# Attention before two MoE layers: one pool of four PSUM banks, an order written out step by step, and a joint tile for the last queries of two heads

## The chip, the cores and the metric

The kernel runs on one core of a Trainium2 chip, in one launch. The metric is the device time of that launch in microseconds. Three runs of the kernel before took 1164.0 us in the median (1159.83 to 1167.98).

## The reference

The inputs are `q`, `k` and `v` of shape (2, 8, 576, 64), and the weights of two mixture-of-experts layers. Only the attention is touched by the change:

```
q_rot, k_rot = (rotate(q), rotate(k))          # rotary embedding, halves of 32
scores = scale * q_rot @ k_rot^T               # scale = 1/8
scores = scores - max(scores)
attn = exp(scores)
attn = attn / (sum(attn) + 1e-09)
out = attn @ v                                 # 2 batches x 8 heads x 576 x 64
```

The output is laid out as 1152 tokens x 512 and goes through the first MoE layer (8 experts, 512 to 1024 to 512, weights from a Sinkhorn iteration) and the second (144 tokens per expert).

## The kernel before, in words

Everything is in fp32 or fp32r. The attention takes the first 180 us or so of the span, and the first MoE layer, the second and the output follow. The 16 (batch, head) pairs are worked on as 8 pairs `P` of two heads `h`; a group `g` = 2P + h is one head. The 576 queries of a head are five tiles, four of 128 queries and one of 64. All 576 keys of a head are scored at once.

For one head the steps are these.

- **Rotation** (`rot`, L1230 to 1254). Four tensor_tensor instructions turn the raw q or k of a pair; they run on GpSimd (`POOL` in the profile), and on VectorE (`DVE`) for the first pair and for the q of the second. q is written twice side by side: the second copy is a DMA on SyncE's queue, or a ScalarE (`ACT`) copy for pair 0.
- **Transposes of q and k** (`tq`, L1267). 15 TensorE (`PE`) transposes fill two PSUM banks called `T`; ACT copies one (L1277) and DVE the other (L1278) to the tile `qk`.
- **Scores of a tile** (`score`, L1282). Two matmuls of 64 rows each write a tile `S` of two banks; an fp32 matmul is two instructions in the trace. DVE takes the negated maximum (L1290), ACT the exponential with its row sum (L1293). There are two `S` tiles, so that the scores of tile n+2 wait for the exponential of tile n.
- **Transposes of the exponentials** (`te`, L1301). Ten transposes of 64 rows fill two `T` banks (five and one bank for the tile of 64 queries); ACT copies the first bank to `pt` (L1311) and DVE the second (L1317).
- **Output** (`pv`, L1319). For a pair, two halves `c` of 288 queries, each five steps over the keys by two heads, into the one bank `PV`; the steps are split three and two. `norm` (L1349) multiplies by the spread reciprocals `rs` on DVE.
- **Reciprocals** (`rcp` L1327, `rbc` L1338). DVE inverts the sums, GpSimd spreads them (for the last pair ACT), nine transposes put them into two `T` banks, and ACT and DVE copy them out. `xsplit` (L1355) splits the result into high and low parts.

Eight PSUM banks are in use: four for the two `S` tiles, three `T` banks that are given out in turn, one `PV`. The order of issue comes from a list of times: within a group each step has a number (`SC` L1463, the tile's index plus 0.1 for `te` and so on), and the steps are issued sorted by it (L1459). `WARM` (L1464) puts filler matmuls of 128x128 by 512 in bf16 into the first steps. Each engine runs its own list in that order.

```
def bank():
    return ps.tile([128, 512], F32, name="T", bufs=3)
...
SC = dict(tq=1.5, rk=0.6, rq=2.6, rcp=4.4, rbc=0.5, pva=2.5, pvb=4.5, n=0.25, xs=0.35)
WARM = (6, 2, 2)
```

The first MoE layer's weights are loaded and converted beside the last pair (`open1`, `wconv`, `WC`), and its first steps (`m1.step`, matmuls of L682 and L701, gate matmuls of L615) stand among the last pieces of the attention.

Of the kernel before, what the change touches and what calls it, by code (L numbers as in the profile page):

```python
# [1134 lines left out]
WC = (0.6, 1.6, 3.6)  # L1135


def attention(tc, nc, ps, pss, lp, q, k, v, rope, ident, xH, xL, m1):
    with ExitStack() as st:
# [56 lines left out]
        tcs = pone.tile([128, 11, 64], F32, name="tcs")  # L1196
        load_k(nc.sync, 0, (0,), False)
# [3 lines left out]
        G.memset(raw["k"][:, :, 4:6, :], 0.0)  # L1201
        G.memset(raw["q"][64:128, :, 4, :], 0.0)
        for t in vs:
            G.memset(t[64:128, 4], 0.0)
        load_k(nc.sync, 0, ())
        load_q(A, 0, ())
        load_k(nc.sync, 0, (1,), False)
        load_q(nc.sync, 0, (1,), False)
        load_v(0)
        load_v(1)  # L1210
        sums = [one.tile([128, 2, 5], F32, name=f"sum{i}") for i in range(2)]
        for t in sums:
            V.memset(t, 1.0)
        wb = one.tile([128, 512], BF, name="wb")
# [8 lines left out]
        def warm(n):  # L1223
            p = ps.tile([128, 512], F32, name="PV", bufs=1)
            for _ in range(n):
                T.matmul(p, wb[:, 0:128], wb, start=True, stop=True)

        T1 = {}

        def rot(P, n, hs=(0, 1), e=G, dup=None):  # L1230
            x, tb = raw[n], tab[n]
            J = SL[n]
            U = 2 if n == "q" else 1
            if hs[0] == 0:
                T1[n, P] = ptwo.tile([128, 2, J, U, HD], F32, name="t1" + n)
                T1[n] = pone.tile([128, 2, J, HD], F32, name="t2" + n)
            t2 = T1[n]
            o = slice(hs[0], hs[-1] + 1)
            t1 = T1[n, P][:, o, :, 0]
# [4 lines left out]
            e.tensor_tensor(t2[:, o, :, 0:32], x[:, o, :, 32:64], table(64, 96), op=OP.mult)  # L1244
# [279 lines left out]
```

## Time and profile before

| | us |
|---|---|
| median of three runs | 1164.0 |
| the profiled execution | 1162.72 |
| its span | 1160.8 |
| PE busy | 1117.1 (96%) |
| DVE busy | 776.6 (67%) |
| ACT busy | 373.0 (32%) |
| POOL busy | 443.1 (38%) |
| first score matmul of pair 0 | at 13.37 |
| first matmul of the first MoE layer | at 178.26 |

How to read it: PE is TensorE's matmuls, PEld its weight loads, which run ahead of the matmuls and so show where TensorE's list stands still. A row of the timeline gives start and duration, engine, source line, what is written from what, the count of merged instructions, and in brackets the idle time before with what ended it. The ends of matmuls are modelled, so that PE shows as busy also while it drains.

### The profile page before, as it was taken

The numbers are of one execution on the slowest core, as the hardware profiler recorded it, in microseconds if no ns is written. First come the engines' busy times: TensorE is split into PE (matmuls) and PEld (weight loads), VectorE is DVE, ScalarE is ACT, GpSimd is POOL, SyncE is SP. The second block draws the span as 40 slices with busy tenths as digits, with TensorE's granted clock in tenths as the row PEclk, the third lists the DMA queues.
The fourth block names the chain that finished last, engine by engine and source line by source line (L and its number), as shares of the span: only waits on it lengthen the run. The fifth ranks groups of instructions, "written<-read, shape, count | busy, mean of one in ns | idle before, by whom it ended". The sixth has DMA issues, their size and how long they took to land. (4 is left out here: it accounts for less than half of the span.)

```text
span 1160.8 us, 20699 instructions
## 1 busy us (share of the span) xinstructions
PE 1117.1 (96%) x8133; PEld 969.4 (84%) x8133; DVE 776.6 (67%) x1732; ACT 373.0 (32%) x853; POOL 443.1 (38%) x429
## 2 busy tenths in 40 slices
PE   5889899999999999999999999999999999999997
PEld 3655557899898888888888898889889887999997
DVE  6677772365667777777777777666678888888200
ACT  4566663223422322223232333223331110222222
POOL 3767515215543443434444354434310000464111
PEclk9799999999999999999999999999999999999999
DMA  3322222200323242232423223111130003978830
GB/s 90 81 54 55 53 85 82 70 1 2 100 64 92 73 123 96 82 91 73 135 83 91 82 93 99 37 37 44 66 134 19 21 1 132 319 256 298 261 98 21
DMA packets 105297, 107.21 MB, mean 92 GB/s; under 512 B 35440, under 2 KB 68592, under 8 KB 105072
## 3 DMA queue, kind: packets, MB, share of 16 engines
q1 hardware_dynamic: 102448, 100.64, 28.0%
q0 software_dynamic: 2048, 4.72, 1.3%
q8 instruction: 64, 1.05, 0.4%
q10 hardware_dynamic: 704, 0.52, 0.2%
q14 instruction: 33, 0.27, 0.1%
HBM read 98.85 MB, written 4.72 MB: 89 GB/s over the span
## 5 line engine op out<-in xcount | busy, mean ns | idle before, releaser
L929 DVE SCALAR_TENSOR_TENSOR acc<-Y,pw,acc 128x512 f32<-128x512 f32 x216 | 158.2, 742 | 1.5 <-PE Y L927 0.4
L865 PE MATMUL T<-xH,wa 128*128 128x256 f32 (+1 forms) x576 | 137.6, 294 | 0.8 <-ACT v L885 0.8
L865 PEld LDWEIGHTS T<-big,wb 128*128 128x128 f32 x864 | 125.8, 188 | 10.7 <-DVE v L878 1.7
L878 DVE TENSOR_TENSOR v<-T,v 128x256 f32<-128x256 f32 (+1 forms) x240 | 108.1, 450 | 38.2 <-PE T L865 35.3
L865 PE MATMUL T<-big,wb 128*128 128x256 f32 (+1 forms) x864 | 133.1, 296 | 0.0
L865 PEld LDWEIGHTS T<-xH,wa 128*128 128x128 f32 x576 | 100.0, 188 | 8.7 <-ACT v L885 3.0
L682 PE MATMUL T<-xH,wa 128*128 128x384 f32 x336 | 93.0, 338 | 0.0
L774 POOL TENSOR_TENSOR wa<-wraw,wa 128x512 fp32r<-128x512 f32 (+1 forms) x48 | 48.8, 1019 | 105.0 <-ACT wa L773 105.0
L865 PE MATMUL T<-xL,wa 128*128 128x256 f32 (+1 forms) x288 | 84.5, 293 | 0.0
L1290 DVE TENSOR_REDUCE negmax<-S 128x1 f32<-128x576 f32 (+1 forms) x80 | 60.2, 752 | 36.2 <-PE S L1288 33.9
L872 DVE SCALAR_TENSOR_TENSOR hlB<-v,hhB 128x320 fp32r<-128x320 f32 x72 | 57.0, 792 | 38.7 <-ACT hhB L871 38.7
L871 ACT ACTIVATE hhB<-v 128x320 fp32r<-128x320 f32 x72 | 34.0, 472 | 136.4 <-DVE v L878 136.4
L871 ACT ACTIVATE hhA<-v 128x256 fp32r<-128x256 f32 x72 | 30.1, 418 | 148.4 <-DVE v L878 148.4
L927 PE MATMUL Y<-wa,hhB 128*128 128x512 f32 x240 | 75.3, 395 | 0.0
L927 PE MATMUL Y<-wb,hhB 128*128 128x512 f32 x240 | 75.1, 394 | 0.0
L872 DVE SCALAR_TENSOR_TENSOR hlA<-v,hhA 128x256 fp32r<-128x256 f32 x72 | 50.6, 703 | 35.3 <-ACT hhA L871 35.3
L1000 DVE SCALAR_TENSOR_TENSOR fr<-fr,fc 128x512 f32<-128x512 f32 x64 | 52.5, 820 | 32.3 <-DMA fr<-in_moe_w 32.3
L793 POOL TENSOR_TENSOR wb<-wraw,wb 128x512 fp32r<-128x512 f32 x24 | 30.6, 1299 | 102.0 <-ACT wb L792 102.0
L701 PE MATMUL Y<-wb,hh 128*128 128x512 f32 x216 | 68.8, 400 | 0.0
L793 POOL TENSOR_TENSOR wa<-wraw,wa 128x512 fp32r<-128x512 f32 x24 | 30.6, 1300 | 99.4 <-ACT wa L792 99.4
L1288 PE MATMUL S<-qk 64*128 64x288 f32 x320 | 62.2, 469 | 4.7 <-ACT big L1293 4.7
L1293 ACT ACTIVATE big<-S,negmax 128x576 f32<-128x576 f32 (+1 forms) x80 | 59.1, 738 | 19.2 <-DVE negmax L1290 15.6
(293 smaller groups left out, 2653.5 us busy)
## 6 DMA issues: line engine op xcount, KB each, us to landing
wraw<-in_moe_w SPq DMA_DIRECT2D x52, 512.0 KB, 5.4
fr<-in_moe_w SPq DMA_DIRECT2D x64, 256.0 KB, 4.1
wraw<-in_moe_w SPq DMA_DIRECT2D x48, 256.0 KB, 3.3
big<-in_moe_w SPq DMA_DIRECT2D x20, 512.0 KB, 4.5
wa<-in_moe_w SPq DMA_DIRECT2D x18, 512.0 KB, 5.0
wb<-in_moe_w SPq DMA_DIRECT2D x14, 512.0 KB, 4.9
fc<-in_moe_w_gate SPq DMA_DIRECT2D x9, 256.0 KB
ysc<-acc SPq DMA_DIRECT2D x9, 256.0 KB, 2.1
```

Source lines behind the costliest of these rows:

```text
L682: nc.tensor.matmul(p[:, :CH], w[:, wi, kt, (fb % 2) * 128:(fb % 2) * 128 + 128], x[:, kt, o], start=(n == 0), stop=(n == 11))
L701: nc.tensor.matmul(self.Y[c][t], a[:, o], w[:, wi, fb % 2], start=(fb == 0 and n == 0), stop=(fb == FB - 1 and n == 2))
L793: G.tensor_tensor(d["W"][:, 1, h], r[:, 2 + h], d["W"][:, 0, h].bitcast(F32), op=OP.subtract)
L865: nc.tensor.matmul(bank[:, 0:n], d[t][:, ww, b, r * 128:(r + 1) * 128], x(xw, r), start=(first and i == 0), stop=(i == 5), skip_group_chec ...
L871: A.activation(HH[:, f, o], src, AF.Relu)
L872: V.scalar_tensor_tensor(HL[:, f, o], src, 0.0, HH[:, f, o].bitcast(F32), op0=OP.max, op1=OP.subtract)
L878: V.tensor_tensor(o, bank[:, 0:n], x, op=OP.add)
L927: nc.tensor.matmul(y, h[:, f, o], w[:, ww, f], start=(f == 0 and z == 0), stop=(f == 1 and z == 2))
L929: V.scalar_tensor_tensor(self.acc[:, t], y, self.pw[:, t, e:e + 1], self.acc[:, t], op0=OP.mult, op1=OP.add)
L1288: T.matmul(p[:, a, :288], QK[g][o, i * 128:(i + 1) * 128], QK[g][o, 640:928], start=True, stop=True)
L1290: V.tensor_reduce(m[0:n], p[0:n, :, :288], axis=AX.XY, op=OP.max, negate=True)
L1293: pexp.append(lambda: A.activation(e[0:n, :576].rearrange("p (a c) -> p a c", a=2), p[0:n, :, :288], AF.Exp, bias=m[0:n], scale=1.0, accum ...
```

## The change

- **One pool of four banks.** The three `T` banks and the `PV` bank are taken once and kept in a list `free`. Every user (`tq`, `te`, `rbc`, each half of the output) takes the bank that was freed first, and gives it back where its copy is issued. While the eighth pair is finished, bank 0 is kept out for the MoE layer.
- **Order written out.** A string `ORDER` names the steps of one turn, one turn per pair; `<` and `>` mean the pair before and the pair after. Maximum, exponential and the two copies are steps of their own. The three-and-two steps of an output half stand between transposes of different tiles. `AFTER` says behind which steps the MoE layer's conversions and its first step are issued.
- **Nine tiles per pair in place of ten.** Tiles 0 to 3 are head 0, tiles 4 to 7 head 1, tile 8 holds the last 64 queries of head 0 in partitions 0 to 63 and of head 1 in 64 to 127. Its scores are four matmuls of 64 rows by 64 columns (L1326). Its maximum, exponential and copies are as for any other tile. The spread of its reciprocals is two 64x64 matmuls in place of a transpose (L1384), and two small copies.
- **First rotations.** Head 0 of pair 0 is rotated on VectorE, then at once head 1's k there and its q on GpSimd; pair 1 is rotated on GpSimd before anything else there, where it was k on GpSimd and q on VectorE among the tiles. The raw q and k have two buffers each. Filler: 14 matmuls at the start in place of 6 and 2, memset on GpSimd, and 2 behind each tile of pair 0.

```diff
-        raw = {n: pone.tile([128, 2, SL[n], HD], F32, name="raw" + n) for n in "qk"}
+        raw = {(n, i): pone.tile([128, 2, SL[n], HD], F32, name=f"raw{n}{i}") for n in "qk" for i in range(2)}
...
-        def bank():
-            return ps.tile([128, 512], F32, name="T", bufs=3)
+        bank = [ps.tile([128, 512], F32, name="T", bufs=3) for _ in range(3)]
+        bank.append(ps.tile([128, 512], F32, name="PV", bufs=1))
+        free = [0, 1, 2, 3]
+        own = []
+        hold = {}
+
+        def take(key, n):
+            hold[key] = [free.pop(0) for _ in range(n)]
+            return [bank[i] for i in hold[key]]
+
+        def give(key, r):
+            if hold[key][r] not in own:
+                free.append(hold[key][r])
...
+        def sc(P, i):
+            p = SS[P, i] = pss.tile([128, 2, 512], F32, name="S")
+            for a in range(2):
+                o = slice(64 * a, 64 * a + 64)
+                if i < 8:
+                    x = QK[P, i // 4]
+                    T.matmul(p[:, a, :288], x[o, i % 4 * 128:i % 4 * 128 + 128], x[o, 640:928], start=True, stop=True)
+                else:
+                    for h in range(2):
+                        x = QK[P, h]
+                        T.matmul(p[64 * h:64 * h + 64, a, :288], x[o, 512:576], x[o, 640:928], start=True, stop=True)
...
+        def rbc(P):
+            p = take(("r", P), 2)
+            d = RD["x", P]
+            for j in range(4):
+                halves(p, j, lambda o: d[o, 2 * j:2 * j + 2].rearrange("p h d -> p (h d)"))
+            for r in range(2):
+                o = slice(64 * r, 64 * r + 64)
+                T.matmul(p[r][o, 256:320], d[o, 8], ident[o, o], start=True, stop=True)
...
-        rot(0, "k", (0,), V)
-        V.memset(wb, 0.0)
-        rot(0, "q", (0,), V, copy)
-        warm(WARM[0])
-        tq(0)
-        rot(0, "k", (1,), V)
-        rot(0, "q", (1,), G, copy)
...
+        rot(0, "k", (0,), V, 0)
+        rot(0, "q", (0,), V, 1)
+        twice(0, 0, True)
+        rot(0, "k", (1,), V, 0)
+        rot(0, "q", (1,), G, 0)
+        load_q(nc.sync, 2, (0, 1))
+        load_k(nc.sync, 2, (0, 1))
+        rq(1)
+        rk(1)
+        warm(WARM[0])
+        for p in range(-1, NP + 3):
+            if p == NP and m1:
+                own = [0]
+                free = [i for i in free if i]
+            for w in ORDER.split():
+                f = w.rstrip("<>")
+                P = p + w.count(">") - w.count("<")
...
+                if f == "tq1" and P == 0:
+                    twice(0, 1, True)
...
+                if x == "te" and P == 0:
+                    warm(WARM[1])
...
-SC = dict(tq=1.5, rk=0.6, rq=2.6, rcp=4.4, rbc=0.5, pva=2.5, pvb=4.5, n=0.25, xs=0.35)
-WARM = (6, 2, 2)
+WARM = (14, 2)
+NC, QB = 9, 3
+ORDER = """sc0 te7< mx0 sc1 pa7< pb7< te8< ex0 pv01<< mx1 pa8< pb8< ex1 tq1 nm0<< lv sc2 qb1 qa1 te0 mx2 sc3 pa0
...
```

The whole order of TensorE in one turn is: sc0 te7 sc1 te8 pv01 tq1 sc2 te0 sc3 te1 pv10 rbc sc4 te2 sc5 te3 pv11 sc6 te4 tq0 sc7 te5 sc8 te6 pv00 (`tq0` for the pair after; te7, te8, `pv` and `rbc` for pairs before). `pv10` is the first three key steps of half 1, `pv11` its last two. ACT's is pa7 ex0 pa8 ex1 qa1 pa0 ex2 pa1 ex3 ra pa2 ex4 pa3 ex5 pa4 ex6 qa0 pa5 ex7 pa6 ex8, and DVE's is mx0 pb7 mx1 pb8 nm0 qb1 mx2 pb0 den mx3 pb1 rb mx4 pb2 mx5 pb3 nm1 mx6 pb4 qb0 mx7 pb5 mx8 pb6 (`pa`, `pb`: the copies of the two banks of a `te`; `qa`, `qb`: those of a `tq`; `ra`, `rb`: those of the spread reciprocals; `mx`, `ex`: maximum, exponential; `nm`: the product with the reciprocals).

TensorE in the middle of a pair, before. `T<-ident,big` is a `te`, `T<-ident,t1q` and `t1k` a `tq`, `T<-ident,rcp` the `rbc`:

```order
L1288 MATMUL S<-qk 128x288 x2
L1265 MATMUL T<-ident,big_100 128x64 x10
L1265 MATMUL T<-ident,rcp 128x64 x9
L1288 MATMUL S<-qk 128x288 x2
L1265 MATMUL T<-ident,big_100 128x64 x10
L1265 MATMUL T<-ident,t1q 128x64 x10
L1265 MATMUL T<-ident,t1k 128x64 x5
L1288 MATMUL S<-qk 128x288 x2
L1265 MATMUL T<-ident,big_99 128x64 x10
```

TensorE after, before the `tq` of a pair's head 1 (here PV and T are two banks of the one pool):

```order
L1322 MATMUL S<-qk 128x288 x2
L1289 MATMUL T<-ident,big_102 128x64 x10
L1361 MATMUL T<-pt_531,big_104 64x288
L1361 MATMUL T<-pt_670,big_104 64x288
L1361 MATMUL T<-pt_531,big_104 64x288
L1361 MATMUL T<-pt_670,big_104 64x288
L1289 MATMUL PV<-ident,t1q 128x64
L1289 MATMUL T<-ident,t1q 128x64
```

Where a `te` was followed at once by `rbc` or `tq`, which take two more of three banks, output matmuls now stand between.

TensorE after, the joint tile of the last queries:

```order
L1322 MATMUL S<-qk 128x288 x2
L1289 MATMUL T<-ident,big_102 128x64 x10
L1326 MATMUL S<-qk 64x288 x4
L1289 MATMUL T<-ident,big_103 128x64
L1289 MATMUL PV<-ident,big_103 128x64
```

Two tiles of `S` with two matmuls each have become one with four of half the width.

VectorE in the first steps, before (the four rotations of head 0's q, the copy of the first `tq`, the rotations of head 1's k):

```order
L1244 TENSOR_TENSOR t2q<-rawq,tabq 128x5x32
L1245 TENSOR_TENSOR t2q<-rawq,tabq 128x5x32
L1246 TENSOR_TENSOR rawq<-rawq,tabq 128x320
L1247 TENSOR_TENSOR t1q<-rawq,t2q 128x5x64
L1278 COPY qk<-T 128x7x64
L1244 TENSOR_TENSOR t2k<-rawk,tabk 128x6x32
L1245 TENSOR_TENSOR t2k<-rawk,tabk 128x6x32
L1246 TENSOR_TENSOR rawk<-rawk,tabk 128x384
L1247 TENSOR_TENSOR t1k<-rawk,t2k 128x384
```

VectorE in the first steps, after:

```order
L1245 TENSOR_TENSOR t1q<-rawq,t_101 128x5x64
L1242 TENSOR_TENSOR t_101<-rawk_97,tabk 128x6x32
L1243 TENSOR_TENSOR t_101<-rawk_97,tabk 128x6x32
L1244 TENSOR_TENSOR rawk_97<-rawk_97,tabk 128x384
L1245 TENSOR_TENSOR t1k<-rawk_97,t_101 128x384
L1307 COPY qk<-T 128x7x64
```

The copy that the first scores need has moved behind the rotation of head 1's k.

## Rows read from the trace of the kernel before

**Rows 1.** The page: busy time, share of the span, instructions of each engine
```profile
PE 1117.1 (96%) x8133; PEld 969.4 (84%) x8133; DVE 776.6 (67%) x1732; ACT 373.0 (32%) x853; POOL 443.1 (38%) x429
```

**Rows 2.** Busy time by stretch (columns: PE, PEld, DVE, ACT, POOL, granted clock, DMA)
```profile
29.00:57.00 28.00, 23.93 (x246) 17.35 (x246) 18.38 (x33) 17.05 (x44) 20.58 (x17) 0.76 0.34 84
57.00:76.80 19.80, 17.81 (x213) 11.62 (x211) 14.04 (x27) 12.84 (x32) 13.05 (x11) 1.00 0.16 36
```

**Rows 3.** Timeline of PE: first scores of pairs 1, 2, 7; first MoE matmul; first gate
```profile
34.09 1.27 PE L1288 MATMUL S<-qk 64*128 64x288 f32 x4
56.96 0.76 PE L1288 MATMUL S<-qk 64*128 64x288 f32 x4
155.83 0.76 PE L1288 MATMUL S<-qk 64*128 64x288 f32 x4
178.26 0.45 PE L682 MATMUL T<-xH,wa 128*128 128x384 f32 x1
192.68 0.33 PE L615 MATMUL T<-xH,gg 128*16 128x384 f32 x1
```

**Rows 4.** Timeline of PE's weight loads over the first head of a pair
```profile
96.50 0.30 PEld L1288 LDWEIGHTS S<-qk 64*128 64x128 f32 x4 [0.44 <-issue]
97.34 0.31 PEld L1288 LDWEIGHTS S<-qk 64*128 64x128 f32 x4
98.33 0.68 PEld L1324 LDWEIGHTS PV<-pt,big 128*64 128x64 f32 x8
99.45 0.30 PEld L1288 LDWEIGHTS S<-qk 64*128 64x128 f32 x4 [0.44 <-ACT big L1293]
100.76 0.60 PEld L1265 LDWEIGHTS T<-ident,rcp 64*128 64x128 f32 x9 [0.38 <-POOL rcp L1334]
101.28 0.31 PEld L1288 LDWEIGHTS S<-qk 64*128 64x128 f32 x4
102.38 0.39 PEld L1265 LDWEIGHTS T<-ident,big 64*128 64x128 f32 x9 [0.60 <-ACT rs L1347]
103.38 0.33 PEld L1265 LDWEIGHTS T<-ident,t1q 64*128 64x128 f32 x8 [0.61 <-ACT pt L1311]
104.75 0.38 PEld L1265 LDWEIGHTS T<-ident,big 64*128 64x128 f32 x9 [0.44 <-ACT qk L1277]
105.20 1.17 PEld L1324 LDWEIGHTS PV<-pt,big 128*64 128x64 f32 x12
106.80 0.30 PEld L1288 LDWEIGHTS S<-qk 64*128 64x128 f32 x4 [0.44 <-issue]
```

**Rows 5.** Waits of PE's weight loads over five pairs (57 to 156): total, times, longest
```profile
PEld T L1265 <- ACT pt L1311: 7.5, 15, 0.7
PEld T L1265 <- ACT qk L1277: 5.5, 10, 0.7
```

**Rows 6.** Groups by line over the same five pairs: maximum, exponential, reading of its sum
```profile
L1290 DVE TENSOR_REDUCE negmax<-S 128x1 f32<-128x576 f32 (+1 forms) x50 | 37.6, 753 | 24.0 <-PE S L1288 21.7 <-PE T L1265 2.2
...
L1293 ACT ACTIVATE big<-S,negmax 128x576 f32<-128x576 f32 (+1 forms) x50 | 36.9, 738 | 6.6 <-DVE negmax L1290 4.1
...
L1293 ACT ACTIVATION_READ_ACCUMULATOR big<-S,negmax 128x1 f32 (+1 forms) x50 | 9.7, 194 | 0.0
```

**Rows 7.** Timeline of the first 18 us: rotations on DVE, first copy, scores 0 to 3
```profile
9.71 1.03 DVE L1247 TENSOR_TENSOR t1q<-rawq,t2q 128x320 f32<-128x320 f32 x1
...
12.44 0.62 DVE L1278 COPY qk<-T 128x448 f32<-128x448 f32 x1 [1.70 <-PE T L1265]
...
13.37 2.29 PE L1288 MATMUL S<-qk 64*128 64x288 f32 x8
13.63 0.56 DVE L1246 TENSOR_TENSOR rawk<-rawk,tabk 128x384 f32<-128x384 f32 x1
...
16.42 0.76 PE L1288 MATMUL S<-qk 64*128 64x288 f32 x4 [0.76 <-ACT big L1293]
...
17.95 0.76 PE L1288 MATMUL S<-qk 64*128 64x288 f32 x4
```

More of the change, by code (lines that the diff above doesn't have):

```diff
@@ L1196, in attention @@
         tcs = pone.tile([128, 11, 64], F32, name="tcs")
+        wb = one.tile([128, 512], BF, name="wb")
         load_k(nc.sync, 0, (0,), False)
@@ L1221, in attention, with rot @@
                          tcs[:, o, 0:32].unsqueeze(2).to_broadcast([128, SL[n], 2, 32]), AF.Copy)
[L1223 to L1226, printed above, removed]
         T1 = {}
-        def rot(P, n, hs=(0, 1), e=G, dup=None):
-            x, tb = raw[n], tab[n]
+        def rot(P, n, hs=(0, 1), e=G, z=0):
+            x, tb = raw[n, P % 2], tab[n]
             J = SL[n]
@@ L1262, in halves, with warm @@
+        def give(key, r):
+            if hold[key][r] not in own:
+                free.append(hold[key][r])
+        def warm(n):
+            for _ in range(n):
+                T.matmul(bank[free[0]], wb[:, 0:128], wb, start=True, stop=True)
+        QK, EB, SS, MX, PT, PV, RS, RD, XN = {}, {}, {}, {}, {}, {}, {}, {}, {}
         def halves(p, s, src):
@@ L1286, in score, with rows, place @@
+        def rows(i):
+            return 128
+        def place(i, r):
+            return (r, 512) if i == 8 else (i // 4, i % 4 * 128 + 64 * r)
+        def sc(P, i):
+            p = SS[P, i] = pss.tile([128, 2, 512], F32, name="S")
             for a in range(2):
                 o = slice(64 * a, 64 * a + 64)
[L1288 to L1290 removed]
@@ new lines, in te, with pc @@
+        def te(P, i):
+            p = take(("e", P, i), rows(i) // 64)
+            for t in range(5):
+                halves(p, t, lambda o: EB[P, i][o, t * 128:(t + 1) * 128])
+        def pc(P, i, r):
+            h, o = place(i, r)
+            if (P, h) not in PT:
+                PT[P, h] = two.tile([128, 5, 576], F32, name=f"pt{h}")
+            d = PT[P, h][:, :, o:o + 64]
+            x = bank[hold["e", P, i][r]][:, 0:320].rearrange("p (t c) -> p t c", c=64)
+            if r == 0 and rows(i) == 128:
+                A.activation(d, x, AF.Copy)
+            else:
+                V.tensor_copy(d, x)
+            give(("e", P, i), r)
@@ L1323, in pv @@
+        def pv(P, c, m):
+            if m == 0:
+                PV[P, c] = take(("v", P, c), 1)[0]
+            for t in range(*((0, 3), (3, 5))[m]):
                 for h in range(2):
-                    T.matmul(PV[c][64 * h:64 * h + 64, :288], vs[P % 2][:, t, h],
-                             PT[2 * P + h][:, t, c * 288:(c + 1) * 288], start=(t == 0), stop=(t == 4))
-        def rcp(P):
-            d = two.tile([128, 2, 5], F32, name="den")
+                    T.matmul(PV[P, c][64 * h:64 * h + 64, :288], vs[P % 2][:, t, h],
+                             PT[P, h][:, t, c * 288:(c + 1) * 288], start=(t == 0), stop=(t == 4))
@@ new lines, in spread, with ra @@
+        def spread(P, r, f):
+            if P not in RS:
+                RS[P] = two.tile([128, 576], F32, name="rs")
+            x, o = bank[hold["r", P][r]], slice(64 * r, 64 * r + 64)
+            f(RS[P][:, 0:512].rearrange("p (s a c) -> p s a c", a=2, c=64)[:, :, r],
+              x[:, 0:256].rearrange("p (s c) -> p s c", c=64))
+            f(RS[P][o, 512:576], x[o, 256:320])
+            give(("r", P), r)
+        def ra(P):
+            spread(P, 0, lambda d, x: A.activation(d, x, AF.Copy))
```

258 lines of the change are left out of this document (90 added, 168 removed).

## The prediction

> **What bounds the kernel now.** I read the page first [rows 1]: TensorE is busy 96% of the span and no other engine over 67%, so that a change pays where it takes work or standstill from TensorE. The execution took 1162.72, 1.9 more than its span; that part I leave as it is. Only the attention changes. The marks of TensorE's timeline [rows 3] divide it: the first score of pair 1 starts at 34.09, of pair 2 at 56.96, of pair 7 at 155.83; the first matmul of the first MoE layer at 178.26, the first gate at 192.68. From pair 2 to pair 7 a pair takes (155.83 - 56.96) / 5 = 19.77 us. In one such stretch [rows 2] TensorE is busy 17.81 of 19.80, DVE 14.04, ACT 12.84, POOL 13.05, at a granted clock of 1.00: no engine is full, so that TensorE's list stands still at times.
>
> Where, is seen in its weight loads [rows 4]. In one head from 96.50 to 106.80 they wait 0.38 for the spread reciprocals (POOL), 0.60 for the copies of the spread out of a T bank, 0.61 for a copy of transposes out of a T bank, and 0.44 for the copy of q and k. Over five pairs the copies `pt` cost 7.5 us and `qk` 5.5 [rows 5]. All but the first are waits for one of three T banks. Prices without a wait come from the same rows, start to start. A score with its ten transposes takes 0.84 (97.34 - 96.50) where a score follows, 0.99 with five transposes where output matmuls follow; where ten are followed by something else, 0.93 (99.45 to 100.38, where the wait for POOL begins). Twelve output instructions take 1.60, eight 1.12, `rbc` 0.52, and `tq` 15 x 0.33 / 8 = 0.62. A head with `rbc` is then 0.84 + 0.99 + 1.12 + 0.93 + 0.52 + 0.93 + 0.62 + 0.93 + 1.60 = 8.48; the other, without `rbc` and with 0.84 for one 0.93, 7.87. Together 16.35 of 19.77: 3.4 us a pair is standstill. A second limit is the two S tiles: score, maximum, exponential and the reading of its sum are 0.76 + 0.75 + 0.74 + 0.19 = 2.44 [rows 4, 6], about 2.5 with the hand-overs, for two tiles.
>
> **The steady pair after.** TensorE's order in one turn has four `te` followed by a score and five by something else: 4 x 0.84 + 5 x 0.93 = 8.01. Output is unchanged, 2 x (1.60 + 1.12) = 5.44; two `tq` 1.24; `rbc` 0.52 and 0.10 for its two small matmuls. The joint tile has as many score instructions as the two short tiles had, one score more than is counted: 0.36. Sum 15.67, 0.7 under before, because five-transpose tiles with a price of 0.99 go.
>
> New are two short stretches with 64 x 64 matmuls (joint tile, end of `rbc`): four more changes of matmul shape a pair. No row shows this change. The nearest bounds are 0 (the changes are hidden) and 0.44, the idle time of the loads behind output matmuls [rows 4]; 0.99 against 0.84 is the nearest whole price, 0.15 a change. I take 0.15: 0.6, bounds 0 and 1.76.
>
> What the loads still wait for: with four banks, one of them with output half of the time, te8 takes a bank of te7 behind one score; before, the same wait with nothing between was 0.61, so 0.61 - 0.36 = 0.25. te2 takes the bank of the spread behind one score, as before 0.60, now with a small DVE copy instead of two of ACT; 0.5. te3 takes te2's bank behind one score: 0.25. Both `tq` and te0 take banks freed before an output piece of 1.12 or a `te`: nothing. The S tiles: between scores of n and n+2 stand 2.45 at the least (6 to 8: 0.93 + 0.62 + 0.9) and mostly 3 to 4, against 2.5; 0.1. Sum 1.1, bounds 0 and four waits of 0.6. rcp: POOL gets it some 1 us before the output piece of 1.60 ends; it needs 0.7, and is hidden; if POOL were late, 0.38 as now. POOL's 13.05 a pair stays and fits in the turn. On SyncE's queue the two DMAs that double q still wait for POOL, with the raw loads behind them; with two raw buffers and a turn between rotation and `tq` nobody waits for either.
>
> DVE loses one maximum (0.75) and one copy, ACT one exponential (0.74 + 0.19) and gains one copy; both stay near 13 and nothing is taken from the time for them. 15.67 + 0.6 + 1.1 = 17.4, a gain of 2.4; five turns from pair 2 to 7: 12.0. Bounds of a turn: 15.7 to 19.8, a gain of 4.1 to 0.
>
> **The start.** Before, the first copy to `qk` runs at 12.44 on DVE and the rotation of head 1's k after it; now the rotation comes first. DVE ends head 0's q at 10.74. A rotation of 384 elements took 0.56 alone, one of 320 took 1.03 while POOL rotated [rows 7]: 1.46 and 3.2 ns an element. The four instructions have 192 + 192 + 384 + 384 = 1152: 1.7 us alone, 3.7 beside POOL. POOL has pair 1's q queued behind head 1's q, so I take 3.7: 14.4, copy 0.62, first score at 15.0, against 13.37. Bounds: 13.1 and 15.0. Scores 0 and 1 took 2.29 together, where one takes 0.76 later: TensorE ran at its lower level. Before, score 2 came 3.05 behind score 0; now the second `tq` stands in front of it, and its q waits on ACT behind the exponential of tile 1: 0.75 + 0.5 for ACT's copy + 1.3 for `tq` at the lower level, score 2 at 20.6 against 16.42. The earlier and longer filler ends before this, with gaps of over 2 us; I therefore take two more tiles at the lower level (score 1.27 [rows 3], with transposes and filler 2.5 each), 25.6, then 1.53 a tile (17.95 - 16.42): scores 5 to 8 by 32.4 with 0.6 for pair 1's `tq`, and with 0.36 for the joint tile pair 1 at 34.3: no gain so far.
>
> But pair 1 then has none of the DVE rotations that stood between tiles. Before it took 22.87, and the granted clock from 29 to 57 is 0.76 in the mean [rows 2]: between the levels of 0.5 and 1.0, half of that time at the lower. Now it takes 17.4 - 1.12 (no earlier output) + 1.2 (two fillers of 0.6) = 17.5: pair 2 starts at 51.8 against 56.96, a gain of 5.2. Bounds: 10 without the lower level in tiles 2 and 3 and with the first score at 13.1, and -1 with another dip of the clock in pair 1.
>
> **The end.** Pair 7 to the MoE layer took 178.26 - 155.83 = 22.43. After: 17.4 - 0.6 (no `tq` of a next pair) + 0.5 (two weight conversions on DVE, one on ACT, in front of the last copies) + te7, te8, 8 output instructions and a wait for the last exponential of 0.9: 0.5 + 0.5 + 1.12 + 0.9 = 20.3, a gain of 2.1. Then, up to the gate, the same matmuls stand in another order, and `rbc` waits for ACT, which has MoE work in front of the spread: 1.1 lost, bounds 0 and 2. Net 1.0. The MoE weights are asked for at pair 7's second `tq`, by this walk 7 us ahead of their first conversion; were they late, DVE would stand still with the maxima behind it, which the 2 us hold.
>
> **The sum.** 5.2 + 12.0 + 1.0 = 18.2 off the profiled execution's 1162.7: 1144.5. The median is 1164.0, 1.3 above it; I keep 1144.5.
>
> **Rivals.**
>
> *Shape changes empty the array.* If each of the four costs the full 0.44, a pair loses 1.16 more, eight pairs 9: 1153.5. For it: loads behind output matmuls idle 0.44 every time [rows 4]. Against it: the matmuls run on meanwhile. The Trainium skill, in "TensorEngine Tiling (Array Packing)", section Tiling Modes, Key Properties, says that a change of tiling mode drains TensorE; by it this rival would hold, and the trace shows the idle loads but no length for a mode of 64 x 64.
>
> *The waits only move.* The bank that frees first is still a copy away, and the exponential's loop binds: a turn of 19.0 in place of 17.4 costs 1.6 x 5 = 8 and pair 1's share 1.6: 1154. Against it: in the order as written each `tq` and `rbc` has output in front.
>
> *TensorE is the bound.* No waits and no shape costs: turns of 15.7 instead of 17.4 gain 1.7 x 6 more, 1134.
>
> *The clock stays down.* This is the slower side. TensorE idles around 8 to 11 and 17 to 19 us in the start as I walk it, and in the kernel before the clock was at its lower level for half of the time from 29 to 57, where TensorE had gaps between tiles [rows 2]. If pairs 1 and 2 run whole at the lower level, each takes 15.7 more, 31 in all: 1176. It decides from 36 us of extra half speed on, which cancels the gain of 18.2. Against it: in the steady part TensorE idles 2 us in 19.8 and the clock is 1.00.
>
> **How the numbers follow.** Forecast 0.62, TensorE the bound 0.12, shape changes 0.12, moved waits 0.07, clock 0.07. One per cent, 11.6 us, is about what a measurement here can tell from no change: 1152.4 is the border. Forecast, TensorE the bound and a part (0.05) of the two middle rivals lie under it: 0.79 faster. The rest of those, 0.14, is within, less 0.01 for the clock rival's milder forms, which make slower 0.08: 0.13 and 0.08. The range runs from 1132 (bounds of start and turn together) to 1157.
>
> **What would show it.** First scores of consecutive pairs 17.4 us apart; loads waiting for `pt`, `qk` and `rs` under 1.3 us a pair in place of 2.6 and more for the first two alone; the first score near 15.0 and pair 2's near 51.8; a joint tile that takes about 0.7 from its score to the next transposes. I am wrong if turns are over 18.5, if the granted clock is under 1.00 beyond pair 1, or if TensorE's loads wait for `rcp` or the MoE conversions.

## The result and the profile after

The changed kernel takes 1134.03 us (median of four runs, 1133.12 to 1136.06) against 1162.95 for the kernel before in the same session: ratio 0.975, 95% interval 0.9712 to 0.9788. The forecast was 1144.5 with a range of 1132 to 1157: faster, as said, and 10.5 us too little. The profiled execution took 1133.12, its span 1131.3, 29.5 less than before.

The page's line of busy time, answering to [rows 1]:

```profile
PE 1103.7 (98%) x8166; PEld 959.8 (85%) x8171; DVE 761.5 (67%) x1715; ACT 367.4 (32%) x846; POOL 449.3 (40%) x443
```

TensorE is busy 13.4 us less in a span that is 29.5 shorter: under half of the gain is work that went (or ran at the lower clock before), the rest is standstill. The busy time by stretch, answering to [rows 2] (same columns; one steady turn):

```profile
45.97:62.47 16.50, 16.37 (x215) 10.91 (x213) 12.88 (x26) 12.05 (x31) 11.53 (x12) 1.00 0.25 58
```

In the steady turn TensorE now lacks 0.13 us of the whole, where it lacked 2.0 of 19.8 (the modelled ends of the matmuls cover the short waits shown below). The marks of TensorE's timeline, answering to [rows 3], with the first score of all in front:

```profile
11.44 1.24 PE L1322 MATMUL S<-qk 64*128 64x288 f32 x8 [1.14 <-DVE qk L1307]
...
28.34 0.76 PE L1322 MATMUL S<-qk 64*128 64x288 f32 x4
...
45.97 0.76 PE L1322 MATMUL S<-qk 64*128 64x288 f32 x4
...
128.46 0.76 PE L1322 MATMUL S<-qk 64*128 64x288 f32 x4
...
147.67 0.45 PE L682 MATMUL T<-xH,wa 128*128 128x384 f32 x1
...
162.76 0.33 PE L615 MATMUL T<-xH,gg 128*16 128x384 f32 x1
```

The first gate comes at 162.76 instead of 192.68, 29.9 earlier: all of the gain lies in the attention. It divides thus:

| stretch | before | after | gain | forecast |
|---|---|---|---|---|
| to pair 2's first score | 56.96 | 45.97 | 10.99 | 5.2 |
| five turns, pair 2 to 7 | 98.87 | 82.49 | 16.38 | 12.0 |
| pair 7 to the first gate | 36.85 | 34.30 | 2.55 | 1.0 |

One steady turn in TensorE's weight loads, answering to [rows 4] (one pair now, not one head; `PV` and `T` are banks of one pool; rows are left out where dots stand):

```profile
78.97 0.30 PEld L1322 LDWEIGHTS S<-qk 64*128 64x128 f32 x4 [0.44 <-ACT big L1336]
...
79.80 0.31 PEld L1322 LDWEIGHTS S<-qk 64*128 64x128 f32 x4
...
80.55 0.14 PEld L1289 LDWEIGHTS T<-ident,big 64*128 64x128 f32 x1 [0.25 <-ACT pt L1351]
...
82.12 0.13 PEld L1289 LDWEIGHTS T<-ident,t1q 64*128 64x128 f32 x1 [0.44 <-DVE pt L1353]
...
82.55 0.36 PEld L1322 LDWEIGHTS S<-qk 64*128 64x128 f32 x4
...
86.06 0.13 PEld L1289 LDWEIGHTS T<-ident,rcp 64*128 64x128 f32 x1 [0.44 <-POOL rcp L1375]
...
86.71 0.30 PEld L1322 LDWEIGHTS S<-qk 64*128 64x128 f32 x4
...
87.64 0.14 PEld L1289 LDWEIGHTS PV<-ident,big 64*128 64x128 f32 x1 [0.44 <-DVE rs L1392]
...
88.64 0.38 PEld L1289 LDWEIGHTS T<-ident,big 64*128 64x128 f32 x9 [0.25 <-ACT pt L1351]
...
90.21 0.30 PEld L1322 LDWEIGHTS S<-qk 64*128 64x128 f32 x4 [0.44 <-issue]
...
91.05 0.40 PEld L1289 LDWEIGHTS T<-ident,t1q 64*128 64x128 f32 x10
...
91.50 0.35 PEld L1322 LDWEIGHTS S<-qk 64*128 64x128 f32 x4
...
92.22 0.13 PEld L1289 LDWEIGHTS T<-ident,big 64*128 64x128 f32 x1 [0.18 <-DVE pt L1353]
...
92.75 0.21 PEld L1326 LDWEIGHTS S<-qk 64*64 64x64 f32 x8
93.40 0.39 PEld L1289 LDWEIGHTS T<-ident,big 64*128 64x128 f32 x10 [0.44 <-DVE negmax L1331]
93.85 0.44 PEld L1361 LDWEIGHTS PV<-pt,big 128*64 128x64 f32 x6
95.46 0.30 PEld L1322 LDWEIGHTS S<-qk 64*128 64x128 f32 x4 [0.44 <-ACT big L1336]
```

Two kinds of brackets stand here. A wait of 0.44 behind output (78.97, 82.12, 86.06, 90.21, 95.46) is idle time of the loads while twelve or eight output matmuls still run; the matmuls lose nothing by it (the output of 93.85 still takes its usual 1.61 to the next score at 95.46, for 1.60 in [rows 4]). The waits that cost are 0.25 at 80.55 and 88.64 (a copy `pt`), 0.44 at 87.64 (the copy of the spread reciprocals), 0.18 at 92.22: about 1.1. Over the stretch from 51 to 134 us the copies, which cost 7.5 and 5.5 in [rows 5], come to this:

```profile
PEld T L1289 <- DVE pt L1353: 2.0, 7, 0.4
PEld T L1289 <- ACT pt L1351: 2.0, 8, 0.3
...
PEld PV L1289 <- DVE pt L1353: 1.1, 3, 0.4
...
PEld PV L1289 <- ACT pt L1351: 0.5, 2, 0.2
```

5.6 in all, part of it idle time behind output, and no wait for `qk` is left.

### The profile page after: what moved, and what is told of

The parts are those of the page before. It is cut to its first block, busy times and chain, and to the rows that moved or that the text cites. A ratio compares the mean times of both kernels' runs of the same rounds, so it can differ in the third digit from the quotient of the medians.

```text
span 1131.3 us, 20907 instructions
## 1 busy us (share of the span) xinstructions
PE 1103.7 (98%) x8166; PEld 959.8 (85%) x8171; DVE 761.5 (67%) x1715; ACT 367.4 (32%) x846; POOL 449.3 (40%) x443
## 5 line engine op out<-in xcount | busy, mean ns | idle before, releaser
L865 PEld LDWEIGHTS T<-xH,wa 128*128 128x128 f32 x576 | 100.0, 188 | 9.8 <-ACT v L885 4.0
L1331 DVE TENSOR_REDUCE negmax<-S 128x1 f32<-128x576 f32 x72 | 53.9, 749 | 15.4 <-PE S L1322 14.6
L682 PEld LDWEIGHTS T<-xH,wa 128*128 128x128 f32 x336 | 61.3, 188 | 2.9 <-issue 0.9
L927 PE MATMUL Y<-wa,hhA 128*128 128x512 f32 x192 | 59.9, 393 | 0.0
```

The source lines that it names most:

```text
L682: nc.tensor.matmul(p[:, :CH], w[:, wi, kt, (fb % 2) * 128:(fb % 2) * 128 + 128], x[:, kt, o], start=(n == 0), stop=(n == 11))
L865: nc.tensor.matmul(bank[:, 0:n], d[t][:, ww, b, r * 128:(r + 1) * 128], x(xw, r), start=(first and i == 0), stop=(i == 5), skip_group_chec ...
L927: nc.tensor.matmul(y, h[:, f, o], w[:, ww, f], start=(f == 0 and z == 0), stop=(f == 1 and z == 2))
L1331: V.tensor_reduce(m[0:n], SS[P, i][0:n, :, :288], axis=AX.XY, op=OP.max, negate=True)
```

## The experiments

The part behind the first gate took 965.4 to 974.4 us in the profiles below, with the granted clock of the stretch from 900 to 980 us between 0.91 and 1.00, whatever was edited in the attention. So each run is read at two marks of its own profile as well: the turn, as the distance between the first weight loads of `rcp` in consecutive turns (19.77 before, 16.50 after), and the first weight load of the first gate (192.51 and 162.59).

| run | turn | gate | median, us | ratio to before, 95% interval |
|---|---|---|---|---|
| changed kernel | 16.50 | 162.59 | 1134.03 | 0.975 [0.9712, 0.9788] |
| own_banks | 17.98 | 174.07 | 1143.57 | 0.9833 [0.9805, 0.9862] |
| ten_tiles | 17.24 | 169.59 | 1142.41 | 0.9847 [0.9813, 0.9881] |
| own_ten | 17.86 | 174.40 | 1147.44 | 0.9881 [0.9855, 0.9906] |
| output_behind | 17.50 | 168.48 | 1137.75 | 0.9796 [0.9773, 0.982] |
| joint_wide | 16.39 | 162.12 | 1133.93 | 0.9746 [0.9722, 0.9771] |
| joint_four | 16.88 | 166.03 | 1135.10 | 0.9778 [0.9755, 0.98] |
| new_start | 19.78 | 188.04 | 1159.38 | 0.9975 [0.9955, 0.9995] |
| two_scratch | 16.50 | 163.78 | 1134.05 | 0.9765 [0.9745, 0.9784] |
| short_filler | 16.50 | 162.93 | 1134.05 | 0.9756 [0.9739, 0.9774] |
| no_tile_filler | 16.50 | 163.16 | 1137.26 | 0.9794 [0.9772, 0.9817] |
| swap_spread | 16.20 | 160.53 | 1131.22 | 0.974 [0.9724, 0.9755] |
| swap_bare | 16.20 | 159.23 | 1133.66 | 0.9751 [0.9729, 0.9773] |

### The pool: own_banks

```diff
-        free = [0, 1, 2, 3]
+        free = [0, 1, 2]
-            hold[key] = [free.pop(0) for _ in range(n)]
+            hold[key] = [3] if key[0] == "v" else [free.pop(0) for _ in range(n)]
```

The filler writes bank 3, and the copies `pa4` and `pb4` are issued ahead of `tq0`, so that there is a bank to take; the order of each engine's own list stays.

> The changed kernel with the pool undone: transposes share three banks, the output keeps a fourth for itself, the order of TensorE is untouched. Theory 'the fourth bank': where no output piece is open, each run of transposes now finds two free banks; with three it waits for a copy of about 0.6 us behind a score that covers all but 0.25 of it. Four to five such places a turn give +1.0 to +1.3 us a turn (17.5 to 17.8 us instead of 16.50), 1142 to 1145 us in all. Rival 'the order alone': output between transposes already covers the copies, turns stay within 0.2 us of 16.50, time within 2 us of 1134.

The waits of the weight loads from 56 to 146 us (total, times, longest) and rows from one turn:

```profile
PEld T L1289 <- ACT pt L1351: 8.9, 25, 0.6
PEld T L1289 <- DVE qk L1307: 4.8, 10, 0.5
```
```profile
91.79 0.33 PEld L1289 LDWEIGHTS T<-ident,rcp 64*128 64x128 f32 x8 [0.44 <-POOL xH L1412]
...
97.52 0.39 PEld L1289 LDWEIGHTS T<-ident,t1q 64*128 64x128 f32 x9 [0.60 <-ACT pt L1351]
...
98.96 0.38 PEld L1289 LDWEIGHTS T<-ident,big 64*128 64x128 f32 x9 [0.50 <-DVE qk L1307]
```

A turn takes 17.98, 1.48 more: the theory of the fourth bank, a little above its 1.0 to 1.3. The waits of [rows 5] are back at nearly the old size, in the new order: `tq` behind a `te` waits 0.60 again (0.61 in [rows 4]).

### The joint tile: ten_tiles

```diff
-            return 128
+            return 64 if i % 5 == 4 else 128
...
-            return (r, 512) if i == 8 else (i // 4, i % 4 * 128 + 64 * r)
+            return i // 5, i % 5 * 128 + 64 * r
...
-NC, QB = 9, 3
+NC, QB = 10, 3
```

with the scores, the copies, the spread and the order written for ten tiles again.

> The changed kernel with the joint tile undone: ten tiles a pair, the two of 64 queries apart again, the pool and the order kept. By the prediction's prices the joint tile saves TensorE next to nothing (two short tiles of 0.99 against 0.93 + 0.36 + 0.10 + 0.60): turns stay at 16.5 to 16.7, 1134 to 1136 us. Rival, from the trace after: the joint tile's scores take 0.65 us to the next transposes where a full tile's take 0.54 to 0.59, so that it is one tile less for some 0.3 us of shape changes: turns 17.0 to 17.2 without it, 1138 to 1140 us.

A turn takes 17.24: the rival's turn holds, and the prediction's prices for the joint tile fall. The time, 1142.41, lies 2.4 above the rival's range; pair 0's spread comes 1.8 later here, at 38.31 for 36.55. What the additional tile brings is seen in the waits from 56 to 146 us and in the loads of one turn:

```profile
PEld S L1321 <- ACT big L1331: 5.5, 10, 0.7
```
```profile
90.04 0.33 PEld L1289 LDWEIGHTS T<-ident,rcp 64*128 64x128 f32 x8 [0.44 <-POOL rcp L1368]
90.28 0.19 PEld L1321 LDWEIGHTS S<-qk 64*128 64x128 f32 x1
...
97.79 0.30 PEld L1321 LDWEIGHTS S<-qk 64*128 64x128 f32 x4 [0.67 <-ACT big L1331]
...
100.39 0.30 PEld L1321 LDWEIGHTS S<-qk 64*128 64x128 f32 x4 [0.44 <-ACT big L1331]
```

Two brackets a turn name an exponential, but the one of 0.44 stands behind twelve output matmuls and costs nothing; the score at 97.79 does wait, 0.67. From the score of tile 8 to the output behind tile 7's transposes it is 2.58 here (96.20 to 98.78), where the joint tile with its transposes takes 1.10 (92.75 to 93.85 above): one tile more costs 1.48, of which 0.67 is the wait at the two `S` tiles. The joint tile gives part of that back. The spread of the reciprocals takes 0.65 with its two small matmuls (86.06 to 86.71 above) and 0.24 here (90.04 to 90.28), 0.41 less; the rest, 0.3, lies in the transposes of tile 2 and of the short tile 9. The turn so gains 0.74 by the joint tile.

### Both undone: own_ten

```diff
-        free = [0, 1, 2, 3]
+        free = [0, 1, 2]
...
-NC, QB = 9, 3
+NC, QB = 10, 3
```

and the rest of the edits of own_banks and ten_tiles.

> The changed kernel with both the pool and the joint tile undone: three banks for transposes, one for the output, ten tiles, in the written-out order. Alone the two cost 1.48 us (17.98) and 0.74 us (17.24) a turn against 16.50. Theory 'two separate gains': they add, a turn takes 18.7 us, and the 1.05 us left to the 19.77 of the kernel before is the place of the output pieces (which measured 1.00 when one was moved): 1150 us. Rival 'one gain counted twice': the ten-tile turn hides the bank waits behind its additional score, 18.0 us, 1144. Rival on the other side: without a joint tile the bank waits double, over 19.3 us, 1154.

A turn takes 17.86. They do not add: the first rival's turn (18.0) is nearest, while the time, 1147.44, lies between its 1144 and the 1150 of the theory. A tile of 64 queries takes one bank and not two. The `tq` behind its five transposes finds two of three banks free and starts at once, where the same `tq` waits 0.60 in own_banks; the copies are then late only one step on:

```profile
96.68 0.14 PEld L1289 LDWEIGHTS T<-ident,t1q 64*128 64x128 f32 x1
...
97.98 0.14 PEld L1289 LDWEIGHTS T<-ident,big 64*128 64x128 f32 x1 [0.38 <-DVE pt L1348]
98.51 0.39 PEld L1289 LDWEIGHTS T<-ident,big 64*128 64x128 f32 x9 [0.40 <-DVE qk L1307]
```

So the turn of 19.77 loses 1.91 by the written-out order (19.77 to 17.86) and 1.36 by pool and joint tile together. The other changes, buffers and rotations, do not shorten it: new_start below has them with the old order and takes 19.78. With three banks the joint tile gives nothing (17.86 to 17.98), with four it gives 0.74; the pool gives 0.62 with ten tiles and 1.48 with nine.

### Output as cover: output_behind

```diff
-te8< ex0 pv01<< mx1 pa8< pb8< ex1 tq1 nm0<<
+te8< ex0 mx1 pa8< pb8< ex1 tq1 pv01<< nm0<<
```

> The changed kernel with one step moved: the last two key steps of the first output half come behind the transposes of q and k of head 1 and no longer between these and the joint tile's transposes. Theory 'output as cover': the transposes of q and k then wait for a copy as in the kernel before (0.61 there), +0.5 to +0.6 us a turn, 16.5 becomes 17.0 to 17.1, 1138 to 1139 us. Rival 'banks are free anyway': 16.5, 1134.

```profile
101.23 0.38 PEld L1289 LDWEIGHTS T<-ident,t1q 64*128 64x128 f32 x9 [0.71 <-ACT pt L1351]
102.93 0.30 PEld L1322 LDWEIGHTS S<-qk 64*128 64x128 f32 x4 [0.44 <-PE PV L1361]
```

A turn takes 17.50, 1.00 more, where 0.5 to 0.6 was expected: the wait is there at 0.71, near the 0.61 of the kernel before. The whole loss lies in this `tq`: from its first load, at 100.38, to the output behind it, at 101.81, it takes 1.43, where it takes 0.44 in the changed kernel (98.61 to 99.05, in the same turn). The 0.28 beside the wait have no bracket: one transpose starts ahead of the wait, and the loads behind it take 0.58 to the output. The place of this one output piece is worth 1.00 a turn; the pool is worth 0.62 or 1.48, the joint tile 0.74 at most.

### The price of the joint tile's shape: joint_wide and joint_four

joint_wide scores the joint tile by two matmuls of head 1 over 128 columns, joint_four by four of 128 columns (the first and the second diff):

```diff
-                    for h in range(2):
-                        x = QK[P, h]
-                        T.matmul(p[64 * h:64 * h + 64, a, :288], x[o, 512:576], x[o, 640:928], start=True, stop=True)
+                    x = QK[P, 1]
+                    T.matmul(p[:, a, :288], x[o, 512:640], x[o, 640:928], start=True, stop=True)
```
```diff
-                        T.matmul(p[64 * h:64 * h + 64, a, :288], x[o, 512:576], x[o, 640:928], start=True, stop=True)
+                        T.matmul(p[:, a, :288], x[o, 512:640], x[o, 640:928], start=True, stop=True)
```

> The changed kernel, the joint tile's scores as two matmuls of 64 rows by 128 columns of head 1 in place of four of 64 by 64; this leaves out the scores of head 0's last 64 queries, so that only the time is read. It prices the shape. Prediction: 0.36 for the extra score and 0.15 for each of two changes of shape, 0.66 us a pair, 1128.7 us. Rival 'changes of shape empty the array' at 0.44: 1.2 us a pair, 1124. Rival, from the trace after: quarter matmuls run side by side, so the extra score costs 0.06, and each change costs the drain of about 0.2: 0.46 a pair, 1130.3 us. Free changes: 1133.5.

> The changed kernel, the joint tile's scores as four matmuls of 64 rows by 128 columns (each head's last 128 columns over the whole tile, head 1's written last) in place of four of 64 by 64; this leaves out the scores of head 0's last 64 queries. Theory 'quarters run side by side': the four small ones took 0.65 us to the next transposes where two of 64 by 128 take 0.54 to 0.59; four of 64 by 128 should take about 1.1, a turn 16.9 to 17.0, 1137 to 1138. Rival, as the prediction priced it: the shape does not matter and the extra score costs 0.36 in either form, turns of 16.5 or, without changes of shape, 16.2: 1132 to 1134.

In joint_wide a turn is 0.11 shorter, not 0.66, 1.2 or 0.46. Its loads at the same place of the turn as the rows from 92.75 above:

```profile
92.75 0.30 PEld L1322 LDWEIGHTS S<-qk 64*128 64x128 f32 x4
93.10 0.58 PEld L1289 LDWEIGHTS T<-ident,big 64*128 64x128 f32 x10
93.75 0.20 PEld L1357 LDWEIGHTS PV<-pt,big 128*64 128x64 f32 x4
```

Either form starts at 92.75, since the score waits for an exponential that ends at 92.61; a change of shape into it is hidden there. Behind it the loads of the next transposes come at 93.40 with 64 x 64 and at 93.10 without, and the output behind them at 93.85 and 93.75. In joint_four the four wide matmuls take 1.25:

```profile
94.67 1.25 PE L1326 MATMUL S<-qk 64*128 64x288 f32 x8
```

and the turn 16.88, as the theory said (16.9 to 17.0): four quarter matmuls take 0.72 (the profile of the changed kernel, at 92.75), no longer than the two halves of a full tile with 0.76, and the extra score of the prediction is nothing. The Trainium skill says as much in "TensorEngine Tiling (Array Packing)", section Tiling Modes, Key Properties: different tiles can run their matmuls in parallel; the trace agrees, with 0.72 against 1.25. The same list says that a change of mode drains TensorE; the trace agrees in that the loads behind the 64 x 64 matmuls wait 0.44. It prices the joint tile's pair of changes at 0.10, the first of them hidden behind the exponential; where nothing hides them, at the end of `rbc`, two small matmuls with their pair of changes cost the 0.41 of ten_tiles.

### The start: new_start, two_scratch, short_filler, no_tile_filler

new_start gives the kernel before the changed rotations, buffers and first filler, and nothing else:

```diff
-        rot(0, "q", (0,), V, copy)
-        warm(WARM[0])
-        tq(0)
-        rot(0, "k", (1,), V)
-        rot(0, "q", (1,), G, copy)
...
+        rot(0, "q", (0,), V, copy, 1)
+        rot(0, "k", (1,), V)
...
+        rot(1, "q")
...
+        rot(1, "k")
...
+        warm(WARM[0])
+        tq(0)
...
-WARM = (6, 2, 2)
+WARM = (14, 2, 2)
```

> The kernel before with only the start of the changed one: two buffers for the raw q and k, one shared scratch tile, the rotations of the first two pairs in the changed order and on the changed engines, the earlier and longer filler. Tiles, banks and order of the rest stay. Theory 'the start is a gain of its own': the spread reciprocals of pair 0 are transposed at 40.0 us before and at 36.6 in the changed kernel, whose turns are shorter; with the old turn and the new start I expect them at 37 to 38 and the rest of pair 1 free of DVE rotations, so that the second turn takes 19.8 instead of 21.2: 4 to 5 us in all, 1157.5 to 1159. Rival 'the new start works only with the new order' (the copies of q and k wait behind head 1's k): within 1 us of before. Rival 'the whole start is worth what the marks show', 11 us: 1152.

The spread reciprocals of pair 0 are transposed at 36.05 (40.02 before), those of pair 1 at 55.18 (61.21): 6.0 gained by then, above the 4 to 5 expected. At the gate 4.5 are left: 0.25 are lost up to the first MoE matmul, whose loads wait 0.68 for converted weights (0.44 before), and 1.3 behind it, where the granted clock is 0.58 from 172 to 176 us (1.00 before, from 178 to 182, in the same matmuls). The time shows 2.7, with an interval of 0.6 to 5.2. Pair 2's first score comes at 50.93 (56.96). So of the 11 us up to pair 2, 6.0 are the start's own; by subtraction 3.3 are one turn in the new form, and 1.7 are left for pair 0 in the new form.

two_scratch lets GpSimd's first rotation go beside VectorE's:

```diff
-            t = t2[:, z:z + len(hs), :J]
+            t = t3 if z == 2 else t2[:, z:z + len(hs), :J]
...
-        rot(0, "q", (1,), G, 0)
+        rot(0, "q", (1,), G, 2)
```

> The changed kernel with one scratch tile more, so that GpSimd's first rotation (head 1's q) no longer waits for VectorE's rotations. Theory 'contention': both engines then rotate at once from 8 us on, VectorE's 320- and 384-element instructions take about 1.0 us instead of 0.5, the first score comes 1.5 to 2.5 us later (13 to 14 instead of 11.4), and the time grows by 1 to 2.5 us. Rival 'POOL's wait is the loss': the second transposes of q and k come earlier by the 3.5 us that POOL waited, the first score stays at 11.4, score 2 comes at 15 instead of 17.9, the time falls by 1 to 2 us.

The end of head 0's q and the first step of head 1's k on VectorE, in the changed kernel and then in two_scratch:

```profile
8.54 0.49 DVE L1245 TENSOR_TENSOR t1q<-rawq,t 128x320 f32<-128x320 f32 x1
8.95 0.35 DVE L1242 TENSOR_TENSOR t<-rawk,tabk 128x192 f32<-128x192 f32 x1
```
```profile
9.18 1.03 DVE L1246 TENSOR_TENSOR t1q<-rawq,t 128x320 f32<-128x320 f32 x1
10.14 1.01 DVE L1243 TENSOR_TENSOR t<-rawk,tabk 128x192 f32<-128x192 f32 x1
```

The same instruction takes 0.49 alone and 1.03 beside GpSimd, the first score comes at 13.28 instead of 11.44, and the gate 1.2 later; the time shows no difference. The place is shown, its price lies under what the times tell apart. In the changed kernel both engines use one scratch tile, so that GpSimd starts only behind VectorE's last rotation, which ends at 10.76. The row names an earlier DMA as what it waited for, but with a scratch tile of its own the same instruction starts at 7.72:

```profile
10.99 0.52 POOL L1242 TENSOR_TENSOR t<-rawq,tabq 128x160 f32<-128x160 f32 x1 [7.53 <-DMA rawk<-in_k]
```

short_filler and no_tile_filler change one number each:

```diff
-WARM = (14, 2)
+WARM = (6, 2)
```
```diff
-WARM = (14, 2)
+WARM = (14, 0)
```

> The changed kernel with 6 filler matmuls at the start instead of 14. Theory 'filler holds the clock': the granted clock is 0.5 from the first transposes to about 20 us, the first two scores take twice as long, score 4 (21.6 us in the changed kernel) comes 1 to 2 us later, and so does the rest. Rival 'the clock is set by the gaps after the filler': no difference beyond 0.5 us at pair 1, since gaps of over 2 us stand between scores in either.

> The changed kernel without the two filler matmuls behind each tile of pair 0, nothing else. Theory 'filler is on the path of pair 0': pair 1's first score comes 1 to 1.5 us earlier (27 us instead of 28.3), and then the wait for GpSimd's spread reciprocals takes it all back: their transposes at 36.5 as in the changed kernel, 1134. Rival 'the filler holds the clock': lower clock in pair 0 or 1, their transposes at 38 or later, 1136.

With the short filler scores 0 and 1 take 2.29 (1.24 in the profile of the changed kernel above), the time is the same and pair 0's spread is transposed at 36.89 (36.55). But all twelve experiments show 2.16 to 2.29 there, the nine with the same start and 14 filler matmuls too, at a granted clock of 0.50 to 0.56 from 10 to 16 us: the profile of the changed kernel is the exception, the filler's length does not decide it, and the first theory falls. In short_filler the granted clock reads 1.00 all the while, and the matmuls last as long as at the lower level; the row alone would have misled.

Without filler between the tiles pair 1's first score comes at 27.46, 0.9 earlier, and TensorE then waits 2.35 for GpSimd:

```profile
36.08 0.27 PE L1289 MATMUL PV<-ident,rcp 64*128 64x64 f32 x1 [2.35 <-POOL rcp L1373]
```

and the busy time of the 4 us behind it (columns as in [rows 2]):

```profile
36.00:40.00 4.00, 3.92 (x42) 3.04 (x42) 2.24 (x5) 1.65 (x5) 3.84 (x6) 0.62 0.33 76
```

The gain is taken back whole (the transposes come at 36.08, for 36.55), and behind this standstill the granted clock falls to 0.62 for 4 us, so that the next turn takes 17.54. The gate comes 0.6 later; the time, 1137.26, is 3.2 longer, and the rest of that lies behind the gate. Each theory was half right: filler stands in the way of pair 0, and covers the wait behind it.

### The order of the two copies of the spread: swap_spread, swap_bare

The first diff is swap_spread, both together swap_bare:

```diff
-rb< ra< te2
+ra< rb< te2
```
```diff
-WARM = (14, 2)
+WARM = (14, 0)
...
-            f = A.copy if P == NP - 1 else G.tensor_copy
+            f = A.copy if P in (0, NP - 1) else G.tensor_copy
```

> The changed kernel with the two copies of the spread reciprocals in the other order, so that the transposes of tile 2 take first the bank that ACT frees and then DVE's. If the wait of 0.44 us for DVE's copy is a loss of about 0.3 us a turn: turns of 16.2 to 16.3 instead of 16.50, 1131.7 to 1132.5 us. Rival 'the wait moves': ACT's copy ends no earlier than DVE's, or the S tiles bind next, 16.45 to 16.5, 1134.

> The changed kernel with the two copies of the spread reciprocals swapped (1131.2 us alone), and without filler between the tiles of pair 0, and with pair 0's reciprocals spread by ACT instead of GpSimd, which is still rotating then. Theory: the filler fills TensorE up to 1.53 us a tile where the S tiles allow 1.27, and the wait of 0.5 to 1.7 us for GpSimd goes: the reciprocals of pair 0 are transposed at 34 to 35 us instead of 36.5, turns stay at 16.2, 1129 to 1130 us. Rival 'GpSimd is the limit': pair 2's q and k come from the same queue, so that the gain is given back at the next transposes of q, 1131. Rival 'the clock needs the filler': the granted clock falls to 0.5 in pair 0 or 1, 1133 or more.

```profile
86.42 0.14 PEld L1289 LDWEIGHTS PV<-ident,big 64*128 64x128 f32 x1 [0.15 <-ACT rs L1396]
```

With ACT's copy first the wait at `te2` is 0.15 instead of 0.44, a turn 16.20, as expected. At the gate 0.3 x 7 = 2.1 us are gained. The time of 1131.22 is the lowest of all, 2.8 under the changed kernel, but the intervals of the two ratios overlap: the gain is shown by the marks and not by the time. swap_bare moves the gate another 1.3 earlier (pair 0's spread at 34.74, its loads waiting 1.36 for ACT's spreading, and 0.5 given back in the next turn, 16.68), but its time of 1133.66, where 1129 to 1130 was expected, has an interval that overlaps both. Whether its gain survives behind the gate stays open.

## Why the prediction was right, and where its sum was short

**The view of the bound.** Right: the gain is standstill of TensorE's list at copies out of banks, read from its weight loads. own_banks and output_behind bring those waits back one by one, with the sizes of [rows 4].

**The turn, 17.4 forecast and 16.50 measured.** The three waits for banks were sized well: te8, te3 and te2 at 0.25, 0.25 and 0.44 for 0.25, 0.25 and 0.5. The fourth term, 0.1 for the `S` tiles, was too small: sc7 with te5 took 1.25 (91.50 to 92.75, the 0.18 for a copy at 92.22 within it) for 0.84 and 0.1, as the score of the joint tile waits for the exponential of tile 6, 2.54 behind its score (90.21 to 92.75), the 2.5 of the two `S` tiles. What failed are three prices of TensorE's work:

- two `tq` at 0.62, 1.24: measured 0.43 (82.12 to 82.55) and 0.45 (91.05 to 91.50). The 0.33 of eight merged loads holds the length of the last one, 0.13 to 0.14 in single rows, and 15/8 counts that almost twice; 0.19 for seven steps gives 0.41 for fifteen.
- the joint tile at 0.93 + 0.36 + 0.30: measured 1.10 (92.75 to 93.85). joint_wide and joint_four show why: quarters run side by side, and the changes of shape cost 0.10, the first of them hidden.
- `rbc` at 0.62 + 0.30: measured 0.65 (86.06 to 86.71). The small matmuls and their changes of shape were priced rightly, 0.10 + 0.30 for the 0.41 of ten_tiles; the 0.52 for the transposes was too dear, 0.24 in ten_tiles.

Less the 0.31 that sc7 with te5 took beyond its price, 0.36 + 0.49 + 0.27 - 0.31 = 0.81 of the 0.9 by which the turn was too long. That the joint tile would save nothing on the path was a consequence of the same prices; ten_tiles puts it at 0.74 a turn.

**The start, 5.2 forecast and 10.99 measured.** Pair 1's number was right, 17.5 forecast and 17.63 measured (28.34 to 45.97), but by luck: the turn in it was priced 0.9 too dear, and TensorE stood still for 1.15 at 36.56, waiting for the spread reciprocals, which the prediction had hidden and whose wait it had named as a sign of being wrong. All of the miss is the arrival of its first score, 34.3 forecast and 28.34 measured. The step that failed first is that both engines rotate at once, in 'DVE ends head 0's q at 10.74' and in 'POOL has pair 1's q queued behind head 1's q, so I take 3.7'. GpSimd waits for the shared scratch tile, which the change shows only in a number: `rot(0, "k", (1,), V, 0)` and `rot(0, "q", (1,), G, 0)` end in the same one. VectorE rotates alone, ends head 0's q at 9.03 and the four instructions at 10.76, 1.7 earlier and then 1.9 shorter than forecast, and the first score comes at 11.44 instead of 15.0, 3.6 of the 6.0. two_scratch shows that the contention is real where both run (13.28). The next is 'score 2 at 20.6', 5.6 behind score 0: it took 4.04 (15.48) in this profile at the higher level, 5.17 in that of swap_spread at the lower one. These 1.1 are no lasting gain, since the spread of pair 0 stands at 36.55 in the one and 36.50 in the other. The last 0.8 lie between score 2 and pair 1 (13.7 forecast, 12.86 measured).

**The end, 1.0 forecast and 2.55 measured.** Pair 7's first score to the first MoE matmul took 19.21 for 20.3 forecast, by the prices of the turn; the stretch to the gate grew by 0.67 for 1.1. The MoE weights were not late.

**Rivals.** 'TensorE is the bound' gave the time (1134) by turns of 15.7 without waits: there are 16.50 with 1.1 of waits, so the number met it and the mechanism did not. The measured time lies 2 us inside the fast end of the range, because all three terms of the sum erred to one side. 'Shape changes empty the array' is refuted at its price of 0.44 a change: 0.11 a turn for the joint tile's two by joint_wide, and 0.41 for the two of `rbc`, their small matmuls included. 'The waits only move' is refuted by turns of 16.50. 'The clock stays down': the lower level does come between 10 and 20 us, and ends before pair 1; no_tile_filler shows its milder form, 1 us by a fall behind a standstill.

## What to carry to other kernels

Price TensorE's short stretches from start to start, where they stand between other work, not from their loads: loads run ahead and idle while matmuls still run. A bank pool, fewer tiles and output as cover can be one gain seen three times: undo them in pairs before adding them up. Where two engines share a scratch tile, look for the order it forces; it can be the order one wants.

## What the runs showed of the hardware

A VectorE instruction over 9 columns, 0.16 us in its other turns, took 1.73 for pair 0, beside a rotation on GpSimd:

```profile
33.73 1.82 POOL L1245 TENSOR_TENSOR t1k<-rawk,t 128x768 f32<-128x768 f32 x1
...
33.84 1.73 DVE L1366 TENSOR_SCALAR den<-sum 128x9 f32<-128x9 f32 x1
...
35.89 0.61 POOL L1373 COPY rcp<-den 128x512 f32<-128x512 f32 x1 [0.34 <-DVE den L1367]
...
36.55 0.14 PEld L1289 LDWEIGHTS PV<-ident,rcp 64*128 64x128 f32 x1 [1.66 <-POOL rcp L1373]
```

It ended at 35.57, where GpSimd's rotation ended (35.55). TensorE's loads waited 1.66 for the reciprocals; of that the late instruction cost 0.34, as GpSimd, which spreads them, rotated until 35.55 itself. In swap_bare, where ACT spreads the reciprocals, the same instruction still took 1.64, beside a rotation from 31.95 to 33.76. The Trainium skill, "SBUF — State Buffer", section Terms, says that VectorE and GpSimd share a port pair which one holds for a whole instruction while the other waits; these rows agree.
